# A new instruction order in the last two fifths of an adaLN, dilated-attention and SwiGLU block

## The chip, the cores and the metric

The kernel runs on one core of a Trainium2 chip. The metric is the device time of one execution in microseconds (us), lower is better. Engines are named as in the profile: PE is the matmul engine and PEld its weight load, DVE the vector engine, ACT the scalar engine, POOL the GpSimd engine, SP the engine that issues nearly all DMAs.

## The reference

The input has one sequence of 2048 rows of 512. A condition vector `c` gives six modulation rows. The first half is a sliding local attention with dilation 2 and eight positions, 32 heads of 16; the second half is a SwiGLU layer with 1792 hidden columns.

```python
mod = (_silu(c) @ w_mod).reshape(c.shape[0], 6, 1, -1)
sa, ca, ga, sb, cb, gb = (mod[:, 0].copy(), ...)
h = _layernorm(x, axis=-1) * (1 + ca) + sa
x = x + ga * _A_ref(h, A_wqkv, A_wo)     # qkv, 8 dilated neighbours, softmax, weighted sum, wo
h = _layernorm(x, axis=-1) * (1 + cb) + sb
x = x + gb * _B_ref(h, B_w1, B_w3, B_w2) # (silu(h @ w1) * (h @ w3)) @ w2
```

## The kernel before

The 2048 rows are 16 tiles T0 to T15 of 128 rows. Each operation of the program is made once with the buffers that it reads and writes, and gets a number. The list `ORDER` holds these numbers in the order in which they are issued; each engine runs its own operations in that order and never out of it. The list `SLOTS` says which buffer of a pool (one of eight PSUM banks, a `hh` or `vsh` buffer, and so on) each value has. `synchronize` then puts a semaphore wait before an operation wherever an operation on another engine has to be done first: because it makes an input, or because it still uses the buffer that is to be written. So the waits follow from the two lists, and nothing else of the program is free.

What the operations are, with the lines that the profile names, and the short names that this document uses:

- Attention of a tile T. Four gather DMAs on SP fetch its 128x4096 window of values from DRAM into a `vsh` buffer (name: *the loads of T*). DVE multiplies them with the weights (L827, *av T*). PE sums over the window in 8 matmuls (L855, *ac T*). ACT copies the bank (L861, *acc copy T*). SP issues a DMA transpose into `sb_ot` (*ot T*). PE multiplies with `wo` in 4 matmuls (L867, *wo T*), and DVE adds the result to `sb_x` with the row sum (L871, *residual T*).
- Softmax weights of a pair of tiles: DVE L794, L796, L797, PE transposes L807 (*at*), ACT copy L811.
- Second layer norm of a pair: POOL makes the negative mean (L586), ACT squares with the row sum (L590), POOL makes the reciprocal root in three steps (L596, L597, L599), ACT normalizes (L601).
- The tile `h` of a SwiGLU group. Groups are T0-1, T2-3, T4-7, T8-11, T12-13 and T14-15 and are called G0 to G5. From G2 on SP issues one DMA transpose for each tile (*h transposes*), and ACT modulates the four 128-column parts in place (L621).
- A SwiGLU unit is one of 14 column blocks of a group: a gate product and an up product on PE (L883, 4 matmuls each; 128x512 for G2 and G3, 128x256 for G4 and G5), SiLU on ACT (L889), product on DVE (L892) into an `hh` buffer.
- Output of a tile: 14 matmuls on PE in two halves of 7 (L921, *z T first* and *z T second*), which read all 14 `hh` buffers of the group; T14 and T15 are done in column halves (L909). DVE adds `sb_x` (L931), SP stores.

Attention of the last tiles and the SwiGLU of the groups before them are interleaved by `ORDER`: PE has something to multiply while DVE, ACT and the DMAs prepare the next attention tile. All DMAs of this stretch are issued by SP, in list order:

```python
for o in todo:
    for d in o.waits:
        e.wait_ge(d.inc[0], d.inc[2])
    ins = o.fn(e)
```

Of the kernel before, what the change touches and what calls it, by code (L numbers as in the profile page):

```python
# [272 lines left out]
def _build(p, A_x, A_wqkv, A_wo, B_w1, B_w3, B_w2, c, w_mod, out):  # L273
# [752 lines left out]
]  # L1026
SLOTS = [
# [19 lines left out]
]  # L1047


# [26 lines left out]
```

## Time and profile before

| what | value |
|---|---|
| time of three runs | 240.87, 241.81, 242.73 us (median 241.81) |
| the profiled execution's own time | 241.33 us |
| its span in the profile | 239.6 us |
| PE busy | 231.9 us (97%) |
| DVE, ACT, POOL busy | 179.2, 138.8, 30.0 us |
| granted PE clock | full in all 40 slices |
| PE idle between 144 and 174 us | 2.41 us |
| PE idle between 174 and 210 us | 0.00 us |
| last matmul ends, last store lands, span ends | 237.08, 239.13, 239.6 us |

The span is what the profiler sees of the program; the execution's own time is 1.7 us longer. All times below are counted from the span's start.

### The profile page before, as it was taken

How to read it: one execution, taken by the hardware profiler on the slowest of the kernel's cores; microseconds unless marked ns; L12 is line 12 of the kernel's file. 1: busy time of each engine (PE TensorE's matmuls, PEld its weight loads, DVE VectorE, ACT ScalarE, POOL GpSimd, SP SyncE). 2: the span in 40 equal slices, each digit the busy share in tenths (PEclk: the TensorE clock that was granted, in tenths of full speed). 3: DMA queues.
4: the chain of work that ended last, by engine and by line, in shares of the span. 5: the costliest groups of instructions: out<-in, count | busy, mean ns of one | idle time of the engine just before them, and what ended most of it. 6: DMA issues, size and time to landing. Idle time of an engine off the chain costs nothing.

```text
span 239.6 us, 4572 instructions
## 1 busy us (share of the span) xinstructions
PE 231.9 (97%) x1806; PEld 135.9 (57%) x1806; DVE 179.2 (75%) x279; ACT 138.8 (58%) x267; POOL 30.0 (13%) x66
## 2 busy tenths in 40 slices
PE   7899999999999999999999999988999999999995
PEld 4676554545688684664444444433374484566774
DVE  5689999999999999999999989381555125234243
ACT  2289577899978737958735792636466043322210
POOL 4434000013002000420005220032020000000000
PEclk9999999999999999999999999999999999999999
DMA  6999999999999995998953995341300700010102
GB/s 210 373 336 309 138 244 299 214 270 310 335 291 255 250 204 168 248 191 240 228 153 90 198 228 58 96 122 36 77 22 12 100 0 0 3 43 2 47 22 66
DMA packets 46317, 38.85 MB, mean 162 GB/s; under 512 B 21704, under 2 KB 37080, under 8 KB 46296
## 3 DMA queue, kind: packets, MB, share of 16 engines
q1 hardware_dynamic: 46288, 38.56, 67.7%
q8 instruction: 14, 0.23, 0.4%
q14 instruction: 7, 0.06, 0.1%
q10 hardware_dynamic: 8, 0.00, 0.0%
HBM read 29.62 MB, written 4.21 MB: 141 GB/s over the span
## 4 chain that ended last, share of the span: by engine, by line
PE 79%; DMA 6%; DVE 5%; SPq 4%; ACT 2%; POOL 2%; issue 1%; DVEq 0%
PE pall L883 36%; PE pall L921 16%; PE pall L691 7%; PE pall L867 6%; DMA sb_x<-in_A_x_dram 5%; SPq L124 4%; PE pall L711 4%; PE pall L752 3%; PE pall L855 3%; PE pall L909 3%; DVE sb_pq L742 2%; DMA sb_ot<-sb_ac 1%; DVE sb_vsh L827 1%; POOL sb_nm L586 1%; DVE sb_st L555 1%
## 5 line engine op out<-in xcount | busy, mean ns | idle before, releaser
L883 PE MATMUL pall<-sb_h,sb_w 128*128 128x256 bf16 (+1 forms) x672 | 102.9, 308 | 1.7 <-ACT sb_sg L889 1.7
L883 PEld LDWEIGHTS pall<-sb_h,sb_w 128*128 128x128 bf16 x672 | 64.8, 98 | 38.1 <-ACT sb_sg L889 2.1
L892 DVE TENSOR_TENSOR sb_hh<-sb_sg,pall 128x256 bf16<-128x256 bf16 (+1 forms) x84 | 40.0, 506 | 37.8 <-PE pall L883 32.6
L889 ACT ACTIVATE sb_sg<-pall 128x256 bf16<-128x256 f32 (+1 forms) x84 | 35.7, 453 | 50.9 <-PE pall L883 49.0
L921 PE MATMUL pall<-sb_w,sb_hh 128*128 128x512 bf16 x196 | 45.1, 379 | 0.0
L742 DVE TENSOR_TENSOR sb_pq<-sb_q,sb_kT 128x4096 bf16<-128x4096 bf16 x16 | 36.4, 2283 | 0.0
L691 PE MATMUL pall<-sb_h,sb_wqkv 128*128 128x512 bf16 (+1 forms) x160 | 31.1, 336 | 0.4 <-DVE sb_st L555 0.4
L921 PEld LDWEIGHTS pall<-sb_w,sb_hh 128*128 128x128 bf16 x196 | 19.1, 98 | 21.2 <-issue 0.4
L827 DVE TENSOR_TENSOR sb_vsh<-sb_vsh,sb_al 128x4096 bf16<-128x4096 bf16 x12 | 27.3, 2285 | 0.0
L621 ACT ACTIVATE sb_h<-sb_h,sb_modc 128x512 bf16<-128x512 bf16 (+1 forms) x24 | 16.5, 742 | 9.5 <-DMA sb_h<-sb_xn 9.5
L691 PEld LDWEIGHTS pall<-sb_h,sb_wqkv 128*128 128x128 bf16 x160 | 14.6, 97 | 12.1 <-DVE sb_st L555 0.6
L931 DVE TENSOR_TENSOR sb_o<-pall,sb_x 128x512 bf16<-128x512 f32 (+1 forms) x18 | 11.1, 625 | 10.0 <-PE pall L921 6.2
L586 POOL TENSOR_SCALAR sb_nm<-sb_sx 128x2 f32<-128x2 f32 x8 | 3.7, 464 | 108.4 <-DVE sb_x L871 108.3
L867 PE MATMUL pall<-sb_wo,sb_ot 128*128 128x512 bf16 x64 | 15.8, 379 | 0.5 <-DMA sb_ot<-sb_ac 0.5
L711 PE MATMUL pall<-sb_wqkv,sb_h 128*128 128x512 bf16 x64 | 16.0, 379 | 0.0
L871 DVE SCALAR_TENSOR_TENSOR sb_x<-pall,sb_x 128x512 bf16<-128x512 f32 x16 | 10.9, 687 | 4.6 <-PE pall L867 4.2
L644 ACT ACTIVATE sb_h<-pall,sb_modc 128x256 bf16<-128x256 bf16 (+1 forms) x18 | 9.9, 611 | 7.5 <-DVE sb_modc L509 6.5
L590 ACT ACTIVATE sb_xn<-sb_x,sb_nm 128x512 bf16<-128x512 bf16 x16 | 11.4, 716 | 4.8 <-POOL sb_nm L586 4.8
L861 ACT ACTIVATE sb_ac<-pall 128x512 bf16<-128x512 f32 x16 | 9.4, 597 | 7.0 <-PE pall L855 6.8
L601 ACT ACTIVATE sb_xn<-sb_x,sb_nb,sb_rs 128x512 bf16<-128x512 bf16 x16 | 12.2, 804 | 1.5 <-POOL sb_nb L599 1.4
L555 DVE BATCH_NORM_STATS2 sb_st<-sb_x 128x6 f32<-128x512 bf16 x16 | 10.5, 680 | 1.4 <-DMA sb_x<-in_A_x_dram 1.4
L701 ACT ACTIVATE sb_kT<-pall 128x512 bf16<-128x512 f32 x16 | 9.6, 606 | 2.8 <-PE pall L691 2.7
(87 smaller groups left out, 206.7 us busy)
## 6 DMA issues: line engine op xcount, KB each, us to landing
sb_vsh<-v_scratch_dram SPq DMA_DIRECT2D x48, 256.0 KB, 5.4
sb_vshx<-v_scratch_dram SPq DMA_DIRECT2D x16, 256.0 KB, 5.1
sb_w<-in_B_w_dram SPq DMA_DIRECT2D x6, 512.0 KB, 7.2
sb_w<-in_B_w_dram SPq DMA_DIRECT2D x6, 384.0 KB, 4.1
v_scratch_dram<-sb_v SPq DMA_DIRECT2D x16, 128.0 KB, 6.0
out_dram<-sb_o SPq DMA_DIRECT2D x14, 128.0 KB, 1.8
sb_wqkv<-in_A_wqkv_dram SPq DMA_DIRECT2D x6, 256.0 KB, 6.5
sb_x<-in_A_x_dram SPq DMA_DIRECT2D x4, 256.0 KB, 6.5
```

Of the source, the lines that this page charges most:

```text
L555: o = p.op("dve", lambda e, T=T: e.bn_stats(st[:, T, :], x_sb[:, T, :]), 595, ("st", T), r=[vx[T]], w=[vs])
L601: p.op("act", lambda e, vn=vn, T=T: e.activation(vn.at[:], x_sb[:, T, :], ACT.Identity, bias=nb[:, T, :], scale=rs[:, NT + T, :]), c_act(5 ...
L621: return e.activation(vh.at[:, ft, 0:n * P], vh.at[:, ft, 0:n * P], ACT.Identity, bias=modc[:, 8 * which + ft:8 * which + ft + 1], scale=m ...
L691: ins = e.matmul(bank(vp)[:, j * n:(j + 1) * n], wqkv[:, t, col:col + P], vh.at[:, t, 0:n], start=(t == ORDER[0] and j == 0), stop=(t == O ...
L711: ins = e.matmul(bank(vp), vh.at[:, t, tt * P:(tt + 1) * P], wqkv[:, t, 2 * D:3 * D], start=(t == ORDER[0]), stop=(t == ORDER[-1]))
L742: return e.tensor_tensor(vp.at[:], in0, in1, ALU.mult)
L827: return e.tensor_tensor(v_w, v_w, a_w, ALU.mult)
L867: ins = e.matmul(bank(vy), vt.at[:, ft, :], wo[:, ft, :], start=(ft == 0), stop=(ft == KT - 1))
L883: ins = e.matmul(bank(vp)[:, 0:n], wt[:, t, fi * P:(fi + 1) * P], vh.at[:, t, 0:n], start=(t == 0), stop=(t == KT - 1))
L889: p.op("act", lambda e: e.activation(vt.at[:, 0:n], bank(vgp)[:, 0:n], ACT.Silu), c_act(n), k, r=[vgp], w=[vt], table="silu")
L892: p.op("dve", lambda e: e.tensor_tensor(vh_.at[:, 0:n], vt.at[:, 0:n], bank(vup)[:, 0:n], ALU.mult), c_dve(n), k, r=[vt, vup], w=[vh_])
L921: ins = e.matmul(bank(vz), vhh[fi].at[:, tt * P:(tt + 1) * P], w2[:, fi, :], start=(fi == 0), stop=(fi == NF - 1))
```

## The change

Only `ORDER` and `SLOTS` differ. The first 137 operations of SP, 262 of PE, 193 of DVE and 172 of ACT stand in the same order; the last of them runs at about 142 us of the span. Every operation, its shape and its count is as before, POOL's order is wholly the same. `SLOTS` also renames PSUM banks in the unchanged part.

```diff
-    557, 816, 560, 801, 840, 827, 870, 871, 555, 872, 568, 556, 595, 817, 876, 828, 873, 829, 865, 875, 577, 877, 878, 850, 854,
-    842, 571, 841, 843, 572, 573, 561, 562, 563, 846, 578, 579, 851, 756, 881, 852, 580, 879, 880, 894, 574, 581, 886, 887, 564,
-    575, 565, 576, 566, 954, 956, 955, 583, 957, 902, 904, 903, 930, 931, 898, 900, 847, 958, 959, 960, 961, 596, 597, 584, 899,
-    585, 582, 586, 598, 963, 901, 587, 588, 918, 932, 933, 855, 856, 962, 888, 890, 844, 966, 965, 599, 589, 590, 857, 889, 591,
+    557, 816, 560, 801, 840, 827, 870, 871, 555, 872, 568, 556, 817, 876, 841, 865, 854, 875, 561, 873, 846, 877, 828, 571, 842,
+    595, 881, 562, 572, 829, 577, 563, 584, 855, 879, 578, 579, 564, 573, 850, 856, 580, 574, 878, 880, 906, 908, 581, 596, 565,
+    566, 575, 576, 954, 857, 585, 907, 583, 909, 918, 919, 894, 582, 586, 843, 956, 955, 957, 886, 887, 958, 756, 898, 587, 588,
+    895, 597, 890, 891, 589, 926, 847, 598, 599, 959, 960, 962, 899, 900, 901, 927, 961, 848, 590, 600, 591, 601, 1032, 910, 920,
...
```

In words, for the stretch after the softmax transpose of T12-13 (PE, 142.02 us in the profile before). "f G3.6" is a gate or up product of block 6 of group G3.

| engine | order before | order after |
|---|---|---|
| PE | f G2.10, z6 first, z7 first, z4 first, z4 second, ac13, ac12, z5 first, z6 second, at T14-15, f G3.3, f G3.1, wo13, wo12, f G3.5 (2), f G3.12, f G3.4 (2), z5 second, ac15, ac14, f G3.9, f G3.12, z7 second, f G3.1, f G3.2, wo14, wo15, then G4 units | z7 first, z5 first, f G2.10, z4 first, ac12, ac13, z7 second, z6 first, at T14-15, f G3.6 (2), wo12, wo13, f G3.9, f G3.3, z4 second, f G3.1, f G3.4, ac14, ac15, f G3.2, f G3.11, z5 second, f G3.4, wo14, wo15, f G3.7, f G3.9, f G3.2, f G3.11, z6 second, then G4 units |
| DVE | product G2.10, sum T14, av13, product G2.13, av12, softmax T14-15, two output adds, residual 13, residual 12, av15, av14, product G3.4 ... | product G2.13, av12, av13, product G2.10, softmax T14-15, one output add, av15, residual 12, residual 13, product G3.6, av14, one output add, product G3.4 ... |
| ACT | normalize T10, copy L811, normalize T11, T9, L621, acc copies 13 and 12, L621 (3), L811, one SiLU, L590 for T13, T12 ... | normalize T10, copy L811, normalize T9, T11, L621, acc copy 12, L621, acc copy 13, L621 (2), L811, two SiLUs, L590 for T13, T12 ... |
| SP | last load of T15, h transposes of T10, T9, T11, ot13, ot12, four loads of T14, h transposes of T13, T12, ot15, ot14, stores | h transposes of T10, T9, T11, last load of T15, one load of T14, ot12, ot13, a store, three loads of T14, ot14, ot15, h transposes of T12, T13, stores |

From 174 us on the units of G4 and G5 and the output halves of T8 to T13 are in a new order too; the last four output pieces are T15, T15, T14, T14 by column halves instead of T15, T14, T14, T15.

56 rows, old and new, of tables (ORDER, SLOTS) are left out of this document.

## The prediction

> **What bounds the kernel now.** I read the page's busy shares, then the busy time by stretch for the part that changes.
>
> ```profile
> PE 231.9 (97%) x1806; PEld 135.9 (57%) x1806; DVE 179.2 (75%) x279; ACT 138.8 (58%) x267; POOL 30.0 (13%) x66
> ...
> 128.00:144.00 16.00, 16.00 (x109) 7.55 (x106) 15.32 (x23) 12.42 (x22) 6.04 (x7) 1.00 0.88 196
> 144.00:174.00 30.00, 27.59 (x154) 11.77 (x153) 18.05 (x22) 13.84 (x25) 3.63 (x4) 1.00 0.35 76
> 174.00:210.00 36.00, 36.00 (x223) 21.56 (x221) 13.55 (x28) 14.85 (x33) 1.30 (x4) 1.00 0.14 23
> ```
>
> The columns after the stretch and its length are busy us (and count) of PE, PEld, DVE, ACT and POOL, then granted clock, DMA share and GB/s. PE sets the time: from 128 to 144 and from 174 to 210 us it has no idle time, and the clock is full. Only 144 to 174 us has any, 30.00 - 27.59 = 2.41 us. Since the change adds and removes no matmul, this is all that an order can win there. PE's timeline says where it lies; the bracket is the idle time before the row and what ended it:
>
> ```profile
> 162.20 1.04 PE L883 MATMUL pall<-sb_h,sb_w 128*128 128x512 bf16 x4 [1.66 <-ACT sb_sg L889]
> ...
> 165.52 0.62 PE L855 MATMUL pall<-sb_vsh,sb_ind 128*32 128x512 bf16 x8 [0.23 <-ACT sb_sg L889]
> ...
> 171.81 1.90 PE L867 MATMUL pall<-sb_wo,sb_ot 128*128 128x512 bf16 x8 [0.51 <-DMA sb_ot<-sb_ac]
> ```
>
> 1.66 + 0.23 + 0.51 = 2.40 us. The first gap waits for a SiLU, which is only the messenger. The timelines of DVE, POOL and ACT show what held ACT:
>
> ```profile
> 157.13 0.69 DVE L871 SCALAR_TENSOR_TENSOR sb_x<-pall,sb_x 128x512 bf16<-128x512 f32 x1 [0.17 <-PE pall L867]
> 157.75 2.29 DVE L827 TENSOR_TENSOR sb_vshx<-sb_vshx,sb_al 128x4096 bf16<-128x4096 bf16 x1
> ...
> 137.88 0.22 POOL L586 TENSOR_SCALAR sb_nm<-sb_sx 128x2 f32<-128x2 f32 x1 [4.84 <-DVE sb_x L871]
> 157.92 2.19 POOL L586 TENSOR_SCALAR sb_nm<-sb_sx 128x2 f32<-128x2 f32 x1 [16.87 <-DVE sb_x L871]
> ...
> 160.14 0.72 ACT L590 ACTIVATE sb_xn<-sb_x,sb_nm 128x512 bf16<-128x512 bf16 x1 [4.14 <-POOL sb_nm L586]
> ```
>
> Residual 12 frees the negative mean of T12-13 just as av15 begins. The same POOL instruction that took 0.22 us at 137.88 takes 2.19 us: it ends at 160.11, after av15 (160.03). ACT sits in front of L590 for 4.14 us, with the SiLU of G3.5 queued behind the two L590; its bank is what the next gate product needs at 160.54. The 0.51 us are ot14, issued by SP as the last of four transposes.
>
> **The change, part by part.**
>
> *1. The POOL collision goes: -1.66 and -0.23 us.* DVE now runs residual 12, residual 13, product G3.6, and only then av14. POOL's L586 follows residual 13 by 0.09 us (as at 174.44 to 174.53), needs 0.22, and product G3.6 covers it with 0.69 us. ACT also has two SiLUs ahead of L590, so no bank waits behind it. The cover is gone if product G3.6 had run earlier; it can't, it stands behind residual 13 in DVE's order. Were L586 late by 2 us all the same, ACT's next item (SiLU G3.1) would be late by that, less the 0.7 us in which it only waits for its matmuls.
>
> *2. ot14 goes ahead of the h transposes: -0.51 us.* SP issues ot14, ot15 and then the h transposes of T12 and T13, which G4 needs 5 us later. This trades for step 4.
>
> So the wall that is taken away is 2.40 us. What could stand up in its place is found by laying PE's new order end to end: 4 matmuls of 128x512 take 0.86 us from start to start (155.20 to 156.93 for 8), an output half 1.51 (6.04 for 28), ac 0.44, at 0.22. An ACT row hands on at its end, with 0.09 us overlap to the next ACT row.
>
> *3. The h tile of G3: +0.45 us (0 to 0.85).* After the at of T12-13 (next start 142.24) PE has five output halves, one product, two ac and one at: 5 x 1.51 + 0.86 + 0.88 + 0.22 = 9.51, so it asks for the first G3 product at 151.75; before it asked at 153.47, since it had one more output half first. That product needs the four L621 of G3. On ACT these are interleaved with both acc copies: 0.81 x 4 + 0.60 x 2 less overlaps = 4.0 us from the first to the end of the last. The first waits for all three transposes (T10, T9, T11).
>
> ```profile
> 164.92 1.20 SPq L124 DMA_TRANSPOSE sb_h<-sb_xn  x1
> ...
> q8 instruction: 14, 0.23, 0.4%
> ...
> 164.92 3.11 SPq L124 DMA_TRANSPOSE sb_h<-sb_xn  x2
> ```
>
> The first row is one transpose, the last that one and the next. One issue takes 1.20 us, and with nothing in the way the landing is 1.15 us behind it (ot13: issued until 151.72, landed at 152.87). With T10 at 142.35 to 143.56, T9 from 143.76 (its L601 ends at 143.74) and T11 behind it, the last lands at 147.45, the L621 end at 151.5, and PE loses nothing. But the q8 row holds 14 packets of 16 KB, and one was on its way from 143.76 for 1.15 us. A transpose being issued across such a packet (the one after 164.92, at 166.17 with a packet at 166.61) took 1.87 us, and an issue that began at 83.34 in a packet's time took 2.14. If T9's issue is held until the packet is through it ends at 146.0, T11 lands at 148.5, and PE loses 0.85. I take the landing that before had for the same last transpose, 148.16: L621 from 148.19, end 152.2, loss 0.45 us.
>
> *4. ot15 with little room: +0.45 us (0 to 1.7).* From 151.75: eight rows of products and wo before ac14 (6.9 us) and one half (1.51) put ac14 at 160.18; ac15 ends at 161.2; then two products, a half, a product and wo14 put wo15 at 166.01. On ACT acc copy 15 stands behind acc copy 14 and two SiLUs, the second of which waits for a product that ends at 162.07: it ends at 163.22. SP issues ot15 until 164.5, landing 165.64: 0.37 us early. All of that moves along with step 3. A packet of 16 KB at the wrong moment costs what it cost before: the transpose issued at 164.92 to 166.13 landed at 168.77, 2.64 us behind its issue and not 1.15; another, issued until 186.69 with a packet at 186.75, 3.2 us. Here that would be 1.15 to 1.7 us of idle PE. The packets came 228 to 256 PE instructions apart in this half (143.76, 166.61, 186.75); the one of 166.61 came at the 1346th matmul, which the new order reaches within z5 second (162.8 to 164.3), so just about here. A coin flip, weighted by how far it has to overlap: 0.45 us.
>
> [...]
>
> *5. From 174 us on: 0.* The same matmuls in a new order; PE had no idle time there, and each 128x256 block asks for 0.87 us of PE against 0.38 of ACT and 0.42 of DVE. The nearest waits are 0.25 to 0.29 us early, as they were at 193 to 197 us before, where nothing stalled. The end is again a half-tile add (0.42) and a store, 2.5 us behind the last matmul. Renamed banks in the unchanged part: the altered waits are for rows that ended before PE got there (nearest 0.03 us, ac10, which waited as long before for ac11). 0, with 0.1 either way.
>
> Sum: -1.89 - 0.51 + 0.45 + 0.45 + 0 = -1.50 us. The profiled execution took 241.33 us (span 239.6 plus 1.7); 239.83 is what it would take. The median of the runs is 0.48 above that execution, so 240.3 us.
>
> **The rivals.**
>
> *Whole gain.* Steps 3 and 4 cost nothing. For it: both are on time by the undisturbed rows. Against it: 0.1 and 0.4 us of room beside landings that scatter by 1.5. 241.81 - 2.40 = 239.4 us.
>
> *A wash.* Both at their upper ends, 0.85 + 1.7 = 2.55 us, give all back: 242.0. It needs packets at both places; at the first one is known to come.
>
> *Slower: the loads of T14 come too late.* SP now issues one load, ot12, ot13, a store and three more loads (until 154.45 with step 3) where before had four in a row; av14 waits for the last. Step by step av14 must start by 158.3 (ac14 at 160.63 less 2.28 and 0.05): the landing decides from there, us for us, and DVE's output add behind av14 adds 0.15 for ac15's bank. Before, the last landed 3.9 us behind its issue (155.59, 159.48), which gives 158.3 here, and with one piece fewer ahead (0.99 us each) 157.3. But a load of T15 took 6.51 us (139.35 to 145.86): 160.96, 2.66 + 0.15 us of idle PE, so -1.50 + 2.81 = +1.3: 243.1. Against it: eight pieces were in flight then, here three.
>
> **How the numbers follow.** Forecast 0.48, whole gain 0.24, wash 0.13, slower 0.15. A measurement of this kernel can tell about 1% (2.4 us) from no change, so over 1% faster is below 239.4: 0.6 of the whole gain and a third of the forecast, as the three runs scatter by 0.9 us: 0.14 + 0.16 = 0.30. Slower by over 1% (above 244.2) is the last rival with a bad step 4: 0.12 with what I have not seen. Within 1% is the rest, 0.58. The range goes from the whole gain with half a us of scatter to the last rival: 238.9 to 243.1.
>
> **What would show it.** Right: L586 near 156 to 157 us takes 0.2 us; PE's gaps at L883 <- ACT sb_sg are gone; small new ones stand before the first G3 product (released by ACT L621) and before wo15 (by DMA sb_ot). Idle time of PE after 144 us is about 0.9 us instead of 2.4. Wrong: a gap before L855 released by DVE sb_vsh (the last rival), any gap after 175 us, or L586 again at 2 us.

## The result, and the profile after

The changed kernel takes 239.99 us (median of 17 runs, 238.77 to 241.99), the kernel before 242.21 us (median of 17 runs, 240.87 to 242.75). The ratio is 0.991, with a 95% interval of 0.9889 to 0.993: about 0.9% or 2.2 us faster. 240.3 us was forecast, within 1% as the likeliest class. Medians, ratios and intervals, here and below, are of the runs in the faster of the two states that executions of this kernel fall into, and a ratio need not be the exact quotient of the two medians.

The page of the profiled execution after (240.36 us, span 238.6), PE's idle time by stretch, and the row of POOL's negative mean:

```profile
PE 232.2 (97%) x1806; PEld 136.7 (57%) x1806; DVE 179.4 (75%) x279; ACT 138.3 (58%) x267; POOL 28.8 (12%) x66
...
L586 POOL TENSOR_SCALAR sb_nm<-sb_sx 128x2 f32<-128x2 f32 x8 | 1.7, 218 | 105.3 <-DVE sb_x L871 105.3
```

```profile
64.00:96.00 32.00, 30.77 (x293) 22.19 (x290) 31.27 (x46) 23.10 (x49) 1.52 (x5) 1.00 1.02 226
...
144.00:174.00 30.00, 29.19 (x161) 12.70 (x160) 18.73 (x24) 17.10 (x32) 3.11 (x7) 1.00 0.41 92
174.00:210.00 36.00, 36.00 (x224) 21.73 (x223) 12.97 (x25) 12.55 (x28) 0.48 (x2) 1.00 0.08 23
```

Eight L586 now take 1.7 us together (3.7 before): none of them meets DVE any more. PE's idle time from 144 to 174 us is 30.00 - 29.19 = 0.81 us, where 2.41 were. The whole of it is one gap, and there is a second one in the part that was not changed (PE's timeline):

```profile
95.54 1.02 PE L867 MATMUL pall<-sb_wo,sb_ot 128*128 128x512 bf16 x4 [1.04 <-DMA sb_ot<-sb_ac]
...
161.42 0.61 PE L855 MATMUL pall<-sb_vsh,sb_ind 128*32 128x512 bf16 x8
...
168.35 1.04 PE L867 MATMUL pall<-sb_wo,sb_ot 128*128 128x512 bf16 x4 [0.81 <-DMA sb_ot<-sb_ac]
```

The first row is wo7, the last wo15. Both wait for a DMA transpose. The first explains why the two profiled spans differ by 1.0 us only (239.6 and 238.6) where the medians differ by 2.2: PE comes 0.94 us late into the changed stretch. To keep that out, I use a length of its own below: *the stretch* is from the start of the at of T12-13 to the end of the last matmul. It was 237.08 - 142.02 = 95.06 us before and is 235.99 - 142.96 = 93.03 us after, 2.03 us less.

The timelines of DVE, POOL and ACT at the place of the old collision, after, one fence each:

```profile
156.57 0.69 DVE L871 SCALAR_TENSOR_TENSOR sb_x<-pall,sb_x 128x512 bf16<-128x512 f32 x1
157.18 0.68 DVE L892 TENSOR_TENSOR sb_hh<-sb_sg,pall 128x512 bf16<-128x512 bf16 x1
158.34 2.29 DVE L827 TENSOR_TENSOR sb_vsh<-sb_vsh,sb_al 128x4096 bf16<-128x4096 bf16 x1 [0.47 <-DMA sb_vsh<-v_scratch_dram]
```

```profile
157.35 0.22 POOL L586 TENSOR_SCALAR sb_nm<-sb_sx 128x2 f32<-128x2 f32 x1 [15.39 <-DVE sb_x L871]
```

```profile
157.43 0.60 ACT L889 ACTIVATE sb_sg<-pall 128x512 bf16<-128x512 f32 x1 [2.86 <-PE pall L883]
157.92 0.71 ACT L590 ACTIVATE sb_xn<-sb_x,sb_nm 128x512 bf16<-128x512 bf16 x1
```

L586 runs in 0.22 us beside product G3.6, a SiLU stands ahead of L590, and av14 waits 0.47 us for its last load. The first two were in the forecast; the third is where its slower rival stands, and here PE does not wait for it (ac14 at 161.42 has no gap). Which of them is worth what, the experiments had to tell.

One thing about reading gaps. A matmul of 128x512 is drawn 379 ns long (mean of the L921 row on the page before), but the next one starts 216 ns after it (8 of them from 155.20 to 156.93 us in PE's timeline before). So a PE gap that the timeline shows as 1.66 us is 1.82 us from start to start. Counted that way the old gaps before G3.4, ac14, the G3.9 product and wo14 are 1.82 + 0.39 + 0.18 + 0.68 = 3.07 us, and the new one before wo15 is 0.97. The difference, 2.10, is close to the stretch's 2.03.

### The profile page after: what moved, and what is told of

Its sections match the earlier page's. It is cut to its first block, busy times and chain, and to the rows that moved or that the text cites. A ratio compares the mean times of both kernels' runs of the same rounds, so it can differ in the third digit from the quotient of the medians.

```text
span 238.6 us, 4560 instructions
## 1 busy us (share of the span) xinstructions
PE 232.2 (97%) x1806; PEld 136.7 (57%) x1806; DVE 179.4 (75%) x279; ACT 138.3 (58%) x267; POOL 28.8 (12%) x66
## 4 chain that ended last, share of the span: by engine, by line
PE 83%; DMA 8%; DVE 3%; SPq 3%; ACT 1%; issue 0%
PE pall L883 40%; PE pall L921 17%; PE pall L691 7%; PE pall L867 5%; DMA sb_x<-in_A_x_dram 5%; PE pall L711 4%; DMA sb_ot<-sb_ac 3%; PE pall L752 3%; SPq L124 3%; PE pall L855 3%; PE pall L909 3%; DVE sb_pq L742 2%; DVE sb_st L555 1%; PE pall L807 1%; DVE sb_xn L576 1%; ACT sb_ac L861 0%
## 5 line engine op out<-in xcount | busy, mean ns | idle before, releaser
L883 PE MATMUL pall<-sb_h,sb_w 128*128 128x256 bf16 (+1 forms) x672 | 102.6, 308 | 0.0
L883 PEld LDWEIGHTS pall<-sb_h,sb_w 128*128 128x128 bf16 x672 | 65.0, 98 | 35.7 <-issue 2.5
L921 PE MATMUL pall<-sb_w,sb_hh 128*128 128x512 bf16 x196 | 44.9, 379 | 0.0
L921 PEld LDWEIGHTS pall<-sb_w,sb_hh 128*128 128x128 bf16 x196 | 19.0, 98 | 21.6 <-DVE sb_hh L892 0.4
L621 ACT ACTIVATE sb_h<-sb_h,sb_modc 128x512 bf16<-128x512 bf16 (+1 forms) x24 | 16.5, 743 | 9.1 <-DMA sb_h<-sb_xn 9.1
L867 PE MATMUL pall<-sb_wo,sb_ot 128*128 128x512 bf16 x64 | 16.0, 379 | 1.9 <-DMA sb_ot<-sb_ac 1.9
L586 POOL TENSOR_SCALAR sb_nm<-sb_sx 128x2 f32<-128x2 f32 x8 | 1.7, 218 | 105.3 <-DVE sb_x L871 105.3
L601 ACT ACTIVATE sb_xn<-sb_x,sb_nb,sb_rs 128x512 bf16<-128x512 bf16 x16 | 12.4, 807 | 0.7 <-POOL sb_nb L599 0.6
L590 ACT ACTIVATE sb_xn<-sb_x,sb_nm 128x512 bf16<-128x512 bf16 x16 | 11.4, 714 | 1.8 <-POOL sb_nm L586 1.8
L721 ACT ACTIVATE sb_v<-pall 128x512 bf16<-128x512 f32 x16 | 9.6, 605 | 2.8 <-PE pall L711 2.8
```

The costliest lines, as they stand in the source:

```text
L601: p.op("act", lambda e, vn=vn, T=T: e.activation(vn.at[:], x_sb[:, T, :], ACT.Identity, bias=nb[:, T, :], scale=rs[:, NT + T, :]), c_act(5 ...
L621: return e.activation(vh.at[:, ft, 0:n * P], vh.at[:, ft, 0:n * P], ACT.Identity, bias=modc[:, 8 * which + ft:8 * which + ft + 1], scale=m ...
L867: ins = e.matmul(bank(vy), vt.at[:, ft, :], wo[:, ft, :], start=(ft == 0), stop=(ft == KT - 1))
L883: ins = e.matmul(bank(vp)[:, 0:n], wt[:, t, fi * P:(fi + 1) * P], vh.at[:, t, 0:n], start=(t == 0), stop=(t == KT - 1))
L921: ins = e.matmul(bank(vz), vhh[fi].at[:, tt * P:(tt + 1) * P], w2[:, fi, :], start=(fi == 0), stop=(fi == NF - 1))
```

## The experiments

Two theories of the gain. Theory 1: the collision of POOL and DVE costs what it delays on ACT, so what is queued on ACT, SP and PE around it decides. Theory 2: the collision by itself is the 1.66 us. And for the loss before wo15: a 16 KB packet of PE's instructions, or the order of SP's queue.

**The collision alone taken out of the kernel before.**

```diff
-575, 565, 576, 566, 954, ... 961, 596, 597,
+575, 565, 596, 576, 566, 954, ... 961, 597,
```

> The kernel before with one DVE item moved: av15 stands ahead of residual 13 and residual 12 instead of behind them, so POOL's L586 for T12-13 no longer meets it (PE, ACT, SP and POOL keep their orders). Theory 1 (the collision costs what it delays on ACT, and what is queued there decides): L586 takes 0.2 us instead of 2.2 and the 1.66 us gap at L883 goes, but POOL's next step L596 now meets av14, the SiLU of G3.4 stands behind L601 on ACT as before, and PE waits about 1.4 us before ac14 instead; the 0.5 us before wo14 stays. About 1.3 us less than before, 240.9 us. Theory 2 (the collision by itself is the cost): PE idle between 144 and 174 us falls from 2.4 to 0.5 us, 1.9 us less than before, 240.3 us.

Measured: 242.07 us against 242.44 of the kernel before on the same chip, ratio 0.9974 (0.9935 to 1.0013); stretch 94.84 us. POOL and PE in its timeline:

```profile
158.07 0.22 POOL L586 TENSOR_SCALAR sb_nm<-sb_sx 128x2 f32<-128x2 f32 x1 [16.88 <-DVE sb_x L871]
159.93 2.17 POOL L596 TENSOR_SCALAR sb_rs<-sb_var 128x2 f32<-128x2 f32 x1 [1.64 <-ACT sb_xn L590]
```

```profile
165.33 0.61 PE L855 MATMUL pall<-sb_vsh,sb_ind 128*32 128x512 bf16 x8 [1.71 <-ACT sb_sg L889]
...
171.74 1.90 PE L867 MATMUL pall<-sb_wo,sb_ot 128*128 128x512 bf16 x8 [0.64 <-DMA sb_ot<-sb_ac]
```

L586 is free (0.22 us), the gap before G3.4 is gone, and only 0.2 us of the stretch is won. POOL's next step, L596, meets av14 instead (2.17 us); L601 is late, the SiLU of G3.4 stands behind it, and PE waits before ac14. The 1.66 us have moved by one step, nearly whole: theory 2 falls. Theory 1 had the place right and the price too low (1.4 us; it was 1.71), and so its 240.9 us for the whole were missed as well.

**The new order on ACT and SP alone, collision kept.**

```diff
-954, 956, 955, 583, 957, 902, 904, 903, 930, 931, 898, 900, 847, 958, 959, 960, 961, 596, 597, 584, 899, 585, 582, 586, 598, 963, 901, 587, 588, ... 962, ... 599, 589,
+954, 902, 903, 956, 955, 583, 957, 904, 930, 931, 898, 899, 900, 847, 958, 959, 596, 597, 584, 585, 582, 586, 901, 587, 598, 588, 599, 589, 960, 961, 963, 962, ...
```

> The kernel before with the new order on ACT and SP alone, in the stretch around the collision: the SiLU of G3.5 ahead of L590, the SiLU of G3.4 and both acc copies ahead of L601, ot15 and ot14 ahead of the h transposes of T13 and T12. DVE and PE keep their orders, so the collision stays. Theory 1: the gaps before G3.4, ac14 and wo14 go (3.1 us from start to start), but L601 and the h transposes come later, and PE, which in the old order turns to G4 right after wo15, waits about 2.7 us for the first G4 product (released by ACT L621); 0 to 0.5 us less than before, 241.7 to 242.2 us. Theory 2: L586 still takes 2.2 us, so the gap stays about where it was; 242.2 us with the gap at L883 <- ACT sb_sg. A third, the one that would make the other orders needless: gaps gone and nothing in their place, 239.5 us.

Measured: 242.20 us against 242.44, ratio 1.003 (0.9998 to 1.0062), so no gain is shown; stretch 94.83 us, 0.2 less than before. **The same with the DVE move of the first experiment as well,** so that DVE, ACT and SP all have the new order around the collision and only PE the old one:

> The kernel before with the new local order on DVE, ACT and SP together and PE's order kept: av15 ahead of the residuals, SiLUs and acc copies ahead of L601, ot15 and ot14 ahead of the h transposes. Theory 1 (PE's order is the third part: it has to hold back G3 products for the time in which the h tile of G4 is made): L586 takes 0.2 us, the gaps before G3.4, ac14 and wo14 are gone, and PE still waits 2 to 3 us before the first G4 product, stretch 94.5 to 95 us, against 95.06 before and 94.83 with ACT and SP alone; whole time 241.7 to 242.8 us. Rival: with the collision gone as well the h tile comes in time, stretch under 93.5 us, 240.5 us or less.

Measured: 242.82 us against 242.32, ratio 1.0008 (0.9974 to 1.0043). PE's timelines of the two at the place where G4 begins, first without and then with the DVE move:

```profile
170.23 1.89 PE L867 MATMUL pall<-sb_wo,sb_ot 128*128 128x512 bf16 x8
174.73 5.51 PE L883 MATMUL pall<-sb_h,sb_w 128*128 128x256 bf16 x44 [2.61 <-ACT sb_h L621]
```

```profile
169.91 1.89 PE L867 MATMUL pall<-sb_wo,sb_ot 128*128 128x512 bf16 x8
174.12 6.05 PE L883 MATMUL pall<-sb_h,sb_w 128*128 128x256 bf16 x35 [2.32 <-ACT sb_h L621]
```

In both the old gaps before G3.4, ac14 and wo14 are gone and one of 2.3 to 2.6 us has come: in the old PE order G4 begins right after wo15, and its h tile isn't there, since L601 now stands behind the acc copies and the h transposes behind ot15 and ot14. The whole time and the stretch (96.07 us) of the last kernel can't be compared with the others, because its granted clock, the last figure but two, is not full behind the new gap:

```profile
144.00:174.00 30.00, 27.54 (x151) 12.00 (x152) 19.72 (x25) 14.79 (x27) 3.39 (x5) 1.00 0.34 80
174.00:210.00 36.00, 35.72 (x208) 21.42 (x212) 12.27 (x24) 14.53 (x33) 1.09 (x3) 0.95 0.13 23
```

In finer stretches it is 0.97 from 172 to 174 us, 0.50 from 174 to 176, 0.68 from 176 to 178 and full again from 178. The fall begins within the gap (171.80 to 174.12). Up to the start of G4 this kernel takes 174.12 - 143.12 = 31.00 us from the start of the at of T12-13, against 173.54 - 142.02 = 31.52 before and 174.73 - 143.44 = 31.29 without the DVE move. So about 0.5 us is won without PE's part, and 1.5 us are lost behind it. The mean granted clock was 0.993 or less in eight of its ten runs and in five of ten without the DVE move, against 11 of 54 of the kernel before; that the gap is the cause was not tested by itself.

So PE's part of the change is needed for the rest of the 2.03 us: between wo15 and G4 it holds back four G3 products and the last half of T6, 4 x 0.86 + 1.51 = 5.0 us of work. What PE's part would do alone was not run.

**The cover taken away in the changed kernel.** Product G3.6 goes behind av14.

```diff
-585, 907, 583, 909, 918, 919, 894, 582, 586, 843,
+585, 907, 583, 918, 919, 894, 582, 586, 909, 843,
```

> The changed kernel with one DVE item moved: product G3.6 stands behind av14 instead of ahead of it, so residual 13 is followed by av14 at once and POOL's L586 meets it again. Theory 1: L586 takes about 2.2 us again, ACT's L590 come 2 us later, but two SiLUs stand ahead of them on ACT and no bank waits, so PE has no new gap over 0.3 us; 239.8 to 240.4 us. Theory 2: the 1.5 to 1.9 us come back, 241.5 to 241.9 us, with a PE gap between 157 and 166 us.

Measured: 240.22 us against 242.44, ratio 0.9906 (0.9859 to 0.9953); stretch 93.15 us. The collision did not come back as expected, so this run does not tell the theories apart (POOL's and DVE's timelines):

```profile
157.72 0.22 POOL L586 TENSOR_SCALAR sb_nm<-sb_sx 128x2 f32<-128x2 f32 x1 [15.49 <-DVE sb_x L871]
```

```profile
159.05 2.29 DVE L827 TENSOR_TENSOR sb_vsh<-sb_vsh,sb_al 128x4096 bf16<-128x4096 bf16 x1 [1.42 <-DMA sb_vsh<-v_scratch_dram]
```

av14 waits for its load until 159.05, and L586 is done by then. Product G3.6 covers L586, but as long as the load lands this late it isn't needed for that.

**The collision brought back for certain.** av15, which has its loads, goes behind residual 12 and 13.

```diff
-581, 596, 565, 566, 575, 576, 954,
+581, 565, 566, 575, 576, 596, 954,
```

> The changed kernel with one DVE item moved: av15 stands behind residual 12 and 13, as in the order before, with product G3.6 and av14 behind it. Its loads and weights are there by then, so av15 starts right behind residual 13 and POOL's L586 must meet it. Theory 1: L586 takes about 2.2 us and ACT's L590 come 2 us later, but no SiLU that PE waits for stands behind them; no PE gap released by ACT sb_sg; instead av14, which now runs behind av15, is 0.4 to 1.2 us late for ac14 (gap at L855 released by DVE sb_vsh). Stretch from the at of T12-13 to the last matmul 93.5 to 94.3 us (93.0 in the changed kernel); whole time 240.4 to 241.5 us. Theory 2: the gap of 1.6 us or more released by ACT sb_sg is back.

Measured: 241.10 us against 242.32, ratio 0.9933 (0.99 to 0.9966); stretch 93.58 us. POOL's and PE's timelines:

```profile
156.83 2.19 POOL L586 TENSOR_SCALAR sb_nm<-sb_sx 128x2 f32<-128x2 f32 x1 [15.40 <-DVE sb_x L871]
```

```profile
161.80 0.61 PE L855 MATMUL pall<-sb_vsh,sb_ind 128*32 128x512 bf16 x8 [0.83 <-DVE sb_vsh L827]
...
168.37 1.04 PE L867 MATMUL pall<-sb_wo,sb_ot 128*128 128x512 bf16 x4 [0.29 <-DMA sb_ot<-sb_ac]
```

L586 is at 2.19 us again, as in the kernel before, and no PE gap is released by ACT's SiLU. The wait before wo15 is there as in the changed kernel, and smaller; what PE loses anew, it loses to av14, which runs 1.1 us later behind av15. This is theory 1 in its plainest form: the same collision costs 1.82 us in the old order and nothing through ACT in the new one.

**Acc copy 15 early.** It goes directly behind acc copy 14 on ACT, in the changed kernel.

```diff
-588, 895, 597, 890, 891, 589, 926, 847, 598, 599,
+588, 597, 598, 895, 890, 891, 589, 926, 847, 599,
```

> The changed kernel with acc copy 15 moved on ACT ahead of the SiLUs of G3.3 and G3.2, directly behind acc copy 14, so that ot15 can be issued directly behind ot14 (about 0.5 to 0.6 us sooner) and lands about 0.9 us ahead of PE. Theory of the 16 KB packet (the landing of ot15 was 2.52 us behind its issue and not 1.15 because a packet of PE's instructions was on its way at 165.9): the gap before wo15 depends on where the packet falls; if it falls on the same PE instruction, ot15 is issued until 165.2 and mostly through by 165.9, gap 0 to 0.5 us, 239.2 to 239.7 us. If instead the second of two transposes in a row is always slow: the landing stays 2.5 us behind the issue, gap 0.4 us. If the SiLU of G3.3 behind it holds a bank, a new gap at G3.4 (released by ACT sb_sg).

Measured: 239.64 us against 242.44, ratio 0.9906 (0.9867 to 0.9946), the same as the changed kernel has; stretch 92.95 us. ot15 was issued until 166.60, with a packet from 166.51, and landed at 169.40, 2.79 us behind its issue. PE still lost 0.71 us before wo15. Sooner alone isn't enough while the packet meets it.

**The packets moved.** Thirty matmuls of one column in the first warm-up (0.96 us together, at 1.24 us of the span) raise PE's instruction count; all orders and waits stay.

```diff
 def mm(e):
+    for _ in range(30 if i == 0 else 0):
+        e.matmul(bank(vw)[:, 0:1], ones[:, 0:P], ones[:, 0:1], start=True, stop=True)
     return e.matmul(bank(vw)[:, 0:256], ones[:, 0:P], ones[:], start=True, stop=True)
```

> The changed kernel with 30 matmuls of one column put into the first warm-up operation of PE, where PE waits for the first loads anyway (about 0.03 us each). All orders and waits stay; only PE's instruction count at any later place is 60 higher, so a 16 KB instruction packet of PE should come some 30 matmuls earlier: about 161 us instead of 165.9 in the stretch after the change, and 4 to 6 us earlier elsewhere. Packet theory: ot15 lands 1.1 to 1.2 us behind its issue, and the gap before wo15 (0.97 us from start to start) falls under 0.2; the stretch from the at of T12-13 to the last matmul falls from 93.0 to 92.1 us. Rival (two transposes in a row, or the order of SP's queue, make ot15 late): landing stays 2.3 to 2.8 us behind and the gap stays. The whole time may go either way by 1 us, since packets also move in the unchanged part.

Measured: 239.32 us against 242.47, ratio 0.986 (0.981 to 0.9911); stretch 92.35 us (92.1 was expected; PE lost 0.2 us between ac12 and ac13). In the DMA view from 165 to 169 us the changed kernel has the packet, and this one hasn't; the last figure of the row of ot15 is the time from the start of its issue to its landing. The views of the changed kernel come first, the DMA view and SP's timeline, then those of this kernel with PE's timeline behind them (its lines are two further down: L869 is L867):

```profile
q1 hardware_dynamic: 1506, 0.37, 83.0%
q8 instruction: 1, 0.02, 1.4%
...
sb_ot<-sb_ac SPq DMA_TRANSPOSE x1, 3.7
```

```profile
164.59 1.19 SPq L124 DMA_TRANSPOSE sb_ot<-sb_ac  x1
```

```profile
q1 hardware_dynamic: 1597, 0.39, 43.3%
...
sb_ot<-sb_ac SPq DMA_TRANSPOSE x1, 2.3
```

```profile
164.62 1.19 SPq L124 DMA_TRANSPOSE sb_ot<-sb_ac  x1
```

```profile
166.54 1.89 PE L869 MATMUL pall<-sb_wo,sb_ot 128*128 128x512 bf16 x8
```

ot15 is issued from 164.62 to 165.80, as in the changed kernel (164.59 to 165.78), and lands 1.11 us behind (166.91) instead of 2.53 (168.30). wo14 and wo15 run in one piece. The packet was at 159.0, so 60 more PE instructions moved it by even more than the 5 us that were expected: it is PE's. SP's order is the same, so the order alone isn't the cause: the packet is what makes ot15 late.

> As the run with 30 small matmuls, with 64 of them: half a block of 256 PE instructions, so that the packets fall about midway between their former places, near 154 and 177 us instead of 143.5 and 165.9. Packet theory: ot15 lands 1.1 to 1.2 us behind its issue, no gap before wo15; the h transposes of G3 are issued in 1.2 to 1.3 us each without a stretched one, but ot12, ot13 or the loads of T14 meet the packet near 154 us. Rival: ot15 as late as before.

(The page before has 1806 matmuls, 1806 weight loads and 14 packets in the q8 row, 258 PE instructions to a packet on average; over its whole trace the packets are 226 to 296 recorded ones apart.) With 64 of them: 240.21 us against 242.47, ratio 0.989 (0.9843 to 0.9938); stretch 92.05 us, ot15 landing 1.10 us behind, no gap before wo15. What the stretch won, other packets took in the unchanged part: PE lost 0.80 us before wo5 and 0.51 before an early product.

**The same in the kernel before.**

> The kernel before with 30 small matmuls in the first warm-up operation, all orders and waits kept. Packet theory: the packet at 166.61 moves to about 162, the h transpose of T13 that landed 2.64 us behind its issue lands 1.1 to 1.2 us behind, the next issue takes 1.26 instead of 1.87 us, ot14 follows 0.6 us sooner and the gap before wo14 (0.68 us from start to start) falls to 0.1; the other gaps (1.82, 0.39, 0.18 us) stay. Rival: ot14 is late for its place as the fourth of four transposes, 0.68 us stay.

Measured: 241.59 us against 242.47, ratio 0.9954 (0.9924 to 0.9983); stretch 94.47 us instead of 95.06. PE's timeline, with line numbers two higher than before (L885 is L883, L869 is L867):

```profile
162.22 1.04 PE L885 MATMUL pall<-sb_h,sb_w 128*128 128x512 bf16 x4 [1.65 <-ACT sb_sg L891]
...
165.55 0.62 PE L857 MATMUL pall<-sb_vsh,sb_ind 128*32 128x512 bf16 x8 [0.23 <-ACT sb_sg L891]
...
171.24 1.90 PE L869 MATMUL pall<-sb_wo,sb_ot 128*128 128x512 bf16 x8
```

The h transpose of T13 landed 1.10 us behind its issue instead of 2.64, the next issue took 1.27 us instead of 1.87, and the 0.51 us before wo14 are gone, while the two gaps of ACT stand where they stood. So the gap of step 2, too, needed a packet. It needed the place of ot14 in SP's queue as well: as the fourth of four it lands at 171.19, only 0.05 us before PE multiplies, while with the new order on ACT and SP it landed at 169.47, 0.76 us before (170.23).

**Both together, twice,** and the changed kernel once more.

> The changed kernel with both: acc copy 15 directly behind acc copy 14 on ACT, and 30 small matmuls in the first warm-up operation. Packet theory: ot15 is issued 0.6 us sooner and lands 1.1 to 1.2 us behind, about 1 us ahead of PE, so that wo15 has no gap even if the packet falls a little off; stretch from the at of T12-13 to the last matmul 92.0 to 92.2 us, against 93.0; whole time 238.8 to 239.8 us. Rival: gap of 0.5 us or more before wo15 stays.

> The run with acc copy 15 early and 30 small matmuls once more, with more rounds, beside the changed kernel on the same chip. Packet theory: no gap before wo15; 0.6 to 1.2 us less than the changed kernel, 2.8 to 3.4 us less than before.

> The changed kernel once more, for a second profile. Packet theory: the packet near 166 us falls within the issue of ot15 or just behind it again, landing 2.3 to 2.8 us behind the issue, 0.5 to 1.1 us of idle PE before wo15; where the packet of 93 to 97 us falls differs from profile to profile, and with it a wait of about 1.2 us before wo7 or wo6. Stretch 92.8 to 93.2 us.

Measured: the first time 239.33 us against 242.47, ratio 0.9858 (0.9807 to 0.991); the second 239.06 against 242.32, ratio 0.9862 (0.9829 to 0.9896), beside the changed kernel with 239.54, ratio 0.9896 (0.9855 to 0.9937). Stretch 92.05 us both times, ot15 landing 1.11 and 1.10 us behind, and wo14 and wo15 in one piece (chain of waits, second time):

```profile
165.00 0.86 PE pall L885 x4
165.86 1.73 PE pall L869 x8
167.59 3.45 PE pall L885 x16
```

This version is the fastest here, by about 0.5 us in the median over the changed kernel, which the intervals do not separate and which is less than the 0.6 to 1.2 us that were expected. In its second profile the changed kernel had the packet at 164.00, within the issue of ot15: the issue took 1.87 us, the landing was 1.11 behind it, and PE lost 0.24 us before wo15; stretch 92.30, both under what was expected. So how much step 4 costs differs from execution to execution: 0.97 and 0.24 in the changed kernel; 0.72 and 0.71 in the runs without the cover and with acc copy 15 early, where the packet began in the last 0.2 us of the issue; 0.45 in the run with the collision, where it began well within the issue.

## Why the prediction was right

- *The wall.* PE's idle time between 144 and 174 us was taken as all that an order could win, and 174 to 210 us as nothing. Right: the stretch lost 2.03 us there, and no gap came after 175 us. The size was read too low, 2.40 us for 3.07, since the idle column leaves out 0.16 us for every gap.
- *Step 1, the POOL collision: -1.89.* The chain (residual, L586, L590, the SiLU behind it, PE) was right, and the gap went. The cause was put too simply. Taking the collision away alone won 0.4 us in the medians and 0.2 in the stretch, within the interval of nothing; bringing it back in the new order gave no SiLU gap. The sentence that two SiLUs now stand ahead of L590 was the larger half of the reason, and that PE holds back G3 products for G4's h tile wasn't in it. The named cover, product G3.6, wasn't needed: av14 waits for its loads.
- *Step 2, ot14: -0.51.* It went, but the place of ot14 was only half of the reason: without the packet at 166.61, which met one of the four transposes, it is gone in the old order too.
- *Step 3, the h tile of G3: +0.45.* Mis-sized; 0 in the profile after. The packet came at 143.46 and stretched the issue of T10 (1.59 us) instead of T9's; T11 landed at 148.66, and the last L621 ended at 152.58, 0.33 us before PE asked. In the run with acc copy 15 early PE lost 0.17 us there, so the place is as tight as it was called.
- *Step 4, ot15: +0.45.* Right in mechanism and place, and about half of what this profile had: 0.97 us. The packet came at 165.90, 0.12 us after the issue, and the landing 2.53 us behind, between the 1.15 and 3.2 that were shown. Over the profiles of the changed kernel it is 0.24 to 0.97. (The trace before has 226 to 256 recorded PE instructions from packet to packet in this half; 228 to 256 was read.)
- *Step 5: 0.* Right.
- *The sum.* -1.50 was forecast for the profiled pair, -2.03 is the stretch: -3.07 + 0.97 and small change, instead of -2.40 + 0.90. A gain and a loss were both read too small, by 0.67 and 0.07. That the loss is so close is luck: 0.45 + 0.45 was forecast, 0 + 0.97 came. The forecast time, 240.3 us, lies nearer to 239.99 than the forecast gain, 1.5 us, to the measured 2.2; that is luck too, since the kernel before has a median of 242.21 us over 17 runs, where the three runs of the forecast had 241.81.
- *The slower rival.* The last load of T14 landed at 158.31, which is 157.37 counted with the old start of the stretch; 157.3 was worked out. DVE waited 0.47 us, PE not at all.

What a packet cost was read where it came. PE's own instructions ran on without a gap across the packets at 143.76, 166.61 and 186.75 us in the profile before. The DMAs beside a packet were late: the landing of ot15 by 1.4 us (2.53 us behind its issue in the changed kernel, 1.11 with the packet moved), the issue that followed the h transpose of T13 by 0.6 us (1.87 us in the kernel before, 1.27 with the packet moved).

## What to carry to other kernels

A gap that a row of the profile puts down to an engine can come from one instruction further back, as the 1.66 us put down to a SiLU came from L590, which had waited 4.14 us for POOL: ask what stands in that engine's queue ahead of the releaser, and whether taking the trigger away only lets the next step meet the same obstacle, as L596 did here (2.17 us). When operations on several engines are reordered together, the part of one or two engines alone may win little, since a new gap opens elsewhere (with ACT and SP alone 0.2 us of the stretch, with a new gap of 2.61 us); lay the other engines' orders end to end and look where the wait turns up next. And leave a DMA transpose on the path some 1.5 us more than its undisturbed landing needs: here that landing was 1.10 to 1.15 us behind the issue, and 2.53 (ot15 after) and 2.64 (the h transpose of T13 before) with a packet in its way.

## What the runs showed of the hardware that was not expected

PE's 16 KB instruction packets did not come at the same time from profile to profile. With the same orders in the unchanged part, the seventh came at 97.51, 97.58 and 97.12 us in three profiles and at 92.98, 93.13 and 93.67 in three others; the changed kernel itself has 92.98 in one profile and 97.12 in the other. (Of the three profiles left, one, in which everything there runs 2 us later, has 99.62; the others have 94.23 and 94.88, and PE lost 0.93 and 0.17 us before wo6.) Where it came at about 93 us ot7 was on its way (in the changed kernel issued until 92.32, landed at 95.41, 3.09 us behind its issue, against 1.11 in the kernel before), and PE lost 1.21 to 1.39 us before wo7. That is more than half of the 2.2 us that the whole change won. I estimate from it that the packets are part of why the 17 runs of one kernel scatter by 1.9 us (before) and 3.2 us (after); no run tests that.
